# A fused attention and mixture-of-experts kernel: the 1e-9 of two softmax sums becomes a column that tensor_reduce adds, and a table that spreads VectorE's routing work over the attention steps is changed

## The chip, the cores and the metric

The kernel runs on one core of a Trainium2 chip. The metric is the device time of one execution in microseconds (us). The engines are called as in the profile: PE is TensorE (PEld its weight loads), DVE is VectorE, ACT is ScalarE, POOL is GpSimd, SP is the engine that issues nearly all DMAs. Each engine runs its own instructions strictly in the order in which they are written.

## The reference

The reference is windowed attention with a few sink keys, and behind it a two-level mixture of experts over the attention's output. Cut to what matters:

```python
scores = where(keep, q @ k.T / sqrt(D), -1e9)      # B=4, H=8, S=768, D=64, window 128, 4 sinks
a = exp(scores - scores.max(-1))
a = a / (a.sum(-1) + 1e-09)                        # first 1e-9
x = (a @ v) as [3072, 512]
for each token: g = argmax of 4 group logits, e = argmax of that group's 4 expert logits
    g_w = softmax(group logits)[g];  e_w = softmax(expert logits)[e]   # each divides by sum + 1e-9
    out = g_w * e_w * (relu(x @ w1[g, e]) @ w2[g, e])                  # 512 -> 1024 -> 512
```

## The kernel before

**Attention.** The 3072 tokens are 24 tiles of 128 rows. One loop (lines 1081 to 1165) runs 26 iterations i, pipelined three deep: iteration i computes the scores of tile i, transposes and multiplies with the values of tile i-1, and transposes back, normalises and computes routing logits of tile i-2. On PE an iteration is: transposes of tile i-1's probabilities (`tp<-ident,pt`), scores (`ps<-kb,qb`), logits (`lg<-wsd,xT`), two more groups of transposes, values (`po<-pu,vv`, `po<-pa,vv`, `po<-spT,svp`). On DVE it is: minima of the negated scores in two halves (`sm,st<-ps,msk`), the normalised output (`xt<-tp,rc`, function `norm`), and in odd iterations also the normalised logits of two tiles (`lw`, `lt`) and the reciprocals of two tiles' sums (`rc`, function `sums`). So an odd iteration has more fixed DVE work than an even one. ACT computes the exponentials with their row sums, and copies out of PSUM; POOL masks the copied probabilities (affine_select, `pu<-pa`, `pa<-pa`), splits the sink columns (`sp`) and, once in six tiles, subtracts for a split of the sink values (`svp`).

**Routing.** Four batches of 6 tiles. The generator `route_batch` (line 344) yields after each DVE operation or two; `routing(k, ...)` (line 865) runs k such units. At the end of each iteration line 1158 runs `UNITS.get(i, REND)` units, so the table `UNITS` (line 60; 6 where it has no entry) says how many routing operations DVE gets in iteration i. A unit that needs PE first (kind "pe") stops the run until the next iteration. The big operations of a batch are `bf` and `af` (one-hot factors, two of each per batch, counted as two units each); their product on PE (`lg<-af,bf` or `ph<-af,bf`) is added to the table `tab`; `select` then picks the token numbers of an expert (`sel`, `idv`, `gidx`, `idz`, `sidx`), from which POOL gathers rows of x (`xg<-xd,gidx`, line 640). The batch with `pick` 0 chooses the first expert r0, the next one chooses r1 and gives r0's third tile of tokens.

**Weights.** Every expert's two matrices come in 8 chunks of 512 KB (`rw<-in_w`). A chunk is rounded by ACT (`whi`) and its rest is subtracted by DVE (`wlo`, about 1.2 us). `prefetch` (line 656) loads, `wjob` (line 675) rounds. In the loop line 1161 loads one chunk in even iterations from `CHOOK`=14 on and in each of the last three; two iterations later ACT rounds its first half, one iteration after that the second half, and `wlo` follows behind `norm_logits` (the call `late()`, line 1151). So `wlo` stands in iterations 17, 18, 21 and 23.

**Hand-over.** Iterations 24 and 25 have no more scores. `early_work` (line 1068) already feeds PE with the first expert part (r0, 256 tokens): two tiles are transposed (`ph<-ident,xg`), then 8 blocks f of layer 1 run (`ph<-un,whi`, `ph<-un,wlo`, 12 matmuls a block), and behind block 5 (`LATE`) r0's third tile is transposed. From there on experts follow one another, each with its layer 1 and layer 2 on PE.

Of the kernel before, what the change touches and what calls it, by code (L numbers as in the profile page):

```python
# [9 lines left out]
F32 = mybir.dt.float32  # L10
# [4 lines left out]
AF = mybir.ActivationFunctionType  # L15
# [41 lines left out]
XLEAD = 9  # L57
PEGAP = 1.6
REND, TSTEP = 6, 16
UNITS = {7: 3, 9: 3, 10: 9, 15: 3, 16: 9, 17: 5, 21: 3, 22: 9, NI - 1: 2}  # L60
HC = 3
LATE = 5
PELAG = 2.0
# [21 lines left out]
SNAP = 1  # L85
SNAPB = 2
DEPTH = 2
CHOOK = 14
PW = G + NE
WARM = 18  # L90
FILL = [8, 10, 6]
# [40 lines left out]
def moe_attention(tc, kqT, vN, vS, nsw, wgx, w1, w2, out):  # L132
    nc = Pinned(tc)
    v = nc.vector
    with ExitStack() as top, ExitStack() as att:
# [15 lines left out]
        def const(shape, dt, name):  # L151
            return cp.tile(shape, dt, name=name)
# [137 lines left out]
        def other_masks():  # L290
# [3 lines left out]
            v.tensor_tensor(snk[0:D], snk[0:D], isu[0:D], ALU.mult)  # L294
            v.tensor_tensor(mc[0:D, 1], mc[0:D, 1], snk[0:D], ALU.add)

        trib = const([P, P], BF16, "trib")
        rev = const([P, 4], F32, "rev")
        edge = const([P, MAXT + 1], F32, "edge")
# [3 lines left out]
        wsd = const([P, NDC, 2, PW], F32, "wsd")  # L303
        nc.gpsimd.memset(wsd, 0.0)
        def late_consts():
            other_masks()
            nc.sync.dma_start(wsb, wgx.rearrange("(c p) n -> p c n", p=P))
            for j in range(2):
                nc.sync.dma_start(wsd[j * D:(j + 1) * D, :, j],
                                  wgx.rearrange("(c j p) n -> j p c n", j=2, p=D)[j])  # L310
            v.tensor_scalar(colm, col, -float(P), None, ALU.add)
            v.tensor_scalar(trib, diff, 0.0, None, ALU.is_lt)
            v.tensor_scalar(rev, col[:, 0:4], -1.0, 4.0, ALU.mult, ALU.add)
            v.tensor_scalar(edge, col[:, 0:MAXT + 1], float(P), None, ALU.mult)
            v.tensor_copy(val, prti)
            for r in range(NE):
                nc.gpsimd.memset(capt[:, r:r + 1], float(CAPT[r]))
                nc.gpsimd.memset(caps[:, r:r + 1], float(CAPT[r] // P))
            v.tensor_scalar(gen[:, 0:1], win, 1.0, None, ALU.is_lt)
            v.tensor_scalar(gen[:, 1:2], win, float(P), None, ALU.is_gt)  # L320
            v.tensor_scalar(gen[:, 2:3], nsk, float(NSK), None, ALU.is_gt)
            v.tensor_reduce(gen[:, 3:4], gen[:, 0:3], AX.X, ALU.max)
# [21 lines left out]
        def route_batch(i0, nb, lt, wk, pt, tab, na, pick=None):  # L344
            def sm(shape, name, dt=F32):
                return wk.tile([P, MAXB] + shape, dt, name=name, bufs=1)[:, 0:nb]
# [7 lines left out]
            m = sm([nk], "rm")  # L354
            v.tensor_reduce(m, lv, AX.X, ALU.max)
            yield
            d = sm([nk, 4], "rd")
            v.tensor_tensor(d, lv, wide(m), ALU.subtract)
            yield
            o5 = sm([nk, 4], "req")  # L360
# [51 lines left out]
            v.tensor_tensor(av, av, val[:, i0:i0 + nb, None].to_broadcast([P, nb, na]), ALU.mult)  # L412
            yield
            s5 = sm([nk], "rs5")
            v.tensor_reduce(s5, d, AX.X, ALU.add)
            yield
            v.tensor_tensor(m[:, :, 0:G], og, s5[:, :, 1:], ALU.mult)
            yield
            v.tensor_reduce(s5[:, :, 1], m[:, :, 0:G], AX.X, ALU.add)
            ss = sm([2], "rss")  # L420
            v.tensor_scalar(ss, s5[:, :, 0:2], 1e-9, None, ALU.add)
            yield
            v.reciprocal(ss, ss)
            cw = wk.tile([P, MAXB, GW], F32, name="cw", bufs=2)[:, 0:nb]
            v.tensor_tensor(cw, ss[:, :, 0:1].to_broadcast([P, nb, GW]), ss[:, :, 1:2].to_broadcast([P, nb, GW]), ALU.mult)
            gates.extend((i0 + n, cw[:, n]) for n in range(nb))
# [284 lines left out]
        def scores(i, g):  # L711
            t = i % NT
            if g == 0:
                env[i] = e = {}
                e["pt"] = wk.tile([P, H, SW], F32, name="pt", bufs=2)
                if i % 2 == 0:
                    env["st"] = wk.tile([P, 2, 2, H], F32, name="st")
                e["st2"] = env["st"]
                e["st"] = e["st2"][:, :, i % 2]
            m = 3 if t else 2  # L720
            for pp in range(2):
                for j, f in ((0, 0), (1, 1), (0, 1), (1, 0)):
                    d, o = slice(j * D, (j + 1) * D), slice(f * D, (f + 1) * D)
                    end = 2 + 2 * t + f
                    nc.tensor.matmul(psb[g][o, 2 * j + pp, (3 - m) * BW:CW], qb[d, i % NQ, 2 * g + pp, o],
                                     kb[d, end - m:end, 2 * g + pp], start=True, stop=True)
# [4 lines left out]
        def maxima(i, g):  # L731
            t = i % NT
            e = env[i]
            if t:
                v.copy_predicated(psb[g][:, :, CW - D:CW], selu[:, None, :].to_broadcast([P, 4, D]), psb[g][:, :, BW - D:BW])
            e["sm", g] = sm = wk.tile([P, 4, SW], F32, name="sm", bufs=2)
            for k in range(4):
                h = head(g, k)
                v.tensor_tensor_reduce(
                    sm[:, k], psb[g][:, k, CW - SW:CW], msk[:, min(t, 2)], -0.125, 3.0e38,  # L740
                    ALU.add, ALU.min, e["st"][:, 0, h:h + 1])

        def exps(i, g):
            e = env[i]
            for k in range(4):
                h = head(g, k)
                nc.scalar.activation(e["pt"][:, h].rearrange("p (b k) -> p b k", b=2)[:, ::-1],
                                     e["sm", g][:, k].rearrange("p (b k) -> p b k", b=2), AF.Exp, bias=e["st"][:, 0, h:h + 1],
                                     scale=-1.0, accum_out=e["st"][:, 1, h:h + 1])

        def sums(i):
            rc = wk.tile([P, 2, H], F32, name="rc")
            v.tensor_scalar(rc, env[i]["st2"][:, 1], 1e-9, None, ALU.add)
            v.reciprocal(rc, rc)
            for j in range(2):
                env[i - 1 + j].update(rc=rc[:, j], rc2=rc)
# [324 lines left out]
        for i in range(NI + 2):  # L1081
            live = i < NI
            a, b = i - 1, i - 2
            mid, old = 0 <= a < NI, 0 <= b < NI
            state["clk"] += 3.0
            if i == NI:
                state.update(gap=0.0, dve=state["clk"])
                sps.close()
                put_gates(MAXB)
                while later:  # L1090
                    gather(*later.pop(0))
                ps_h = fl.enter_context(tc.tile_pool(name="ps_h", bufs=4, space=PSUM, side="right", reuse_waits="tile"))
                tail.append(ps_h)
                next(ew)
                next(ew)
                if half:
                    half.pop()()()
            if live:
                load_v(i)
            if i == 1:  # L1100
                scores(i, 0)
                scores(i, 1)
            if mid or old:
                env["tp"] = pair()
            if mid:
                trans(a)
                evac(a, 0)
                evac(a, 1)
            if live and i != 1:
                scores(i, 0)  # L1110
            if later and not gates:
                gather(*later.pop(0))
            late = None
            if live:
                if i != 1:
                    scores(i, 1)
                issue()
                warm(FILL[i] if i < len(FILL) else 0, ob[0][:, 224:416])
                late = half.pop()() if half else wjob()
                if half and i % NT == 0:  # L1120
                    late = lambda more=half.pop(): more()()
            if old:
                logits(b)
            if mid:
                sink_t(a)
            if old:
                natural(b)
            if live:
                maxima(i, 0)
                exps(i, 0)  # L1130
            else:
                routing(TSTEP, (None,))
                next(ew, None)
            if mid:
                sink_evac(a)
            if live:
                maxima(i, 1)
                exps(i, 1)
                sink_split(i)
            if i == 0:  # L1140
                late_consts()
            if i % NT == (4 if i else 0) and i < NI - NT + (not i):
                split_s((i + 2) // NT)
            state["clk"] += 3.0
            if old:
                norm(b)
            routing(1, ("pe",))
            if old:
                norm_logits(b)
            if late:  # L1150
                late()
            if mid:
                values(a, 0)
                values(a, 1)
                sink_values(a)
                out_evac(a)
            put_gates(2 if live else MAXB)
            routing(UNITS.get(i, REND) if live else TSTEP, (None, "rd"))
            if live and i % 2:
                sums(i)  # L1160
            if i >= CHOOK and (i % 2 == 0 or i > NI - 4):
                prefetch(min(RAW, len(raws) + (1 if live else RAW)))
            if not live:
                wjob()
                next(ew, None)
# [283 lines left out]
```

## Time and profile before

| | us |
|---|---|
| median of 3 runs (lowest, highest) | 515.48 (514.57, 516.71) |
| the profiled execution | 515.45 |
| span of the profile | 513.7 |
| busy: PE, DVE, ACT, POOL | 495.2, 386.6, 343.9, 160.6 |

The span is what the profiler saw from the first to the last instruction; the profiled execution's own time is 1.75 us longer. Attention ends near 160 us of the span, the experts take the rest. A busy PE in this profile can hide waits, since the ends of matmuls are modelled; the length of a stage is a safer measure.

### The profile page before, as it was taken

Reading aid. Unit: us, or ns where it says so; the run is one execution under the profiler, and the core shown is the slowest. Engines: PE = TensorE matmul, PEld = TensorE weight load, DVE = VectorE, ACT = ScalarE, POOL = GpSimd, SP = SyncE. Lnnn points to the kernel's source line nnn. Section 1 sums busy time; section 2 is a strip of 40 time slices with the busy share of each in tenths; the row PEclk is TensorE's granted clock in tenths of the full one; section 3 lists DMA queues with packets and bytes.
Section 4 is the critical chain, followed back from the end, with each engine's and each line's share of the span. In section 5 each row is a group of like instructions: output and inputs, shape, how many; then the busy total and the mean of one; then the engine's idle time right before and its main releaser. Section 6 shows DMA issues by size and latency. Waiting matters only on the chain. (4 is left out here: it accounts for less than half of the span.)

```text
span 513.7 us, 14666 instructions
## 1 busy us (share of the span) xinstructions
PE 495.2 (96%) x5399; PEld 421.0 (82%) x5399; DVE 386.6 (75%) x1183; ACT 343.9 (67%) x877; POOL 160.6 (31%) x272
## 2 busy tenths in 40 slices
PE   7999999998898999999999999999999999999995
PEld 5788888787687988989888878787779788988884
DVE  7476898898999789985175669847888898788840
ACT  4888878787795445674275667845887887687731
POOL 3464463464365011513304022321253032302101
PEclk9999999999999999999999999999999999999998
DMA  6766775695785645897128379858889797869300
GB/s 199 236 216 218 248 231 183 195 324 178 261 282 150 227 127 173 294 328 266 61 82 301 122 285 305 275 192 286 265 264 323 283 312 229 298 218 332 110 25 27
DMA packets 50000, 114.71 MB, mean 223 GB/s; under 512 B 9486, under 2 KB 9486, under 8 KB 49920
## 3 DMA queue, kind: packets, MB, share of 16 engines
q1 hardware_dynamic: 45424, 100.14, 58.8%
q0 software_dynamic: 4352, 13.26, 7.4%
q8 instruction: 44, 0.72, 0.6%
q10 hardware_dynamic: 144, 0.29, 0.2%
q14 instruction: 36, 0.29, 0.2%
HBM read 100.89 MB, written 13.24 MB: 222 GB/s over the span
## 5 line engine op out<-in xcount | busy, mean ns | idle before, releaser
L102 DVE TENSOR_TENSOR wlo<-rw,whi 128x1024 fp32r<-128x1024 f32 x128 | 153.1, 1218 | 36.5 <-ACT whi L102 35.9
L102 PE MATMUL po<-whi,un 128*128 128x512 f32 (+3 forms) x448 | 148.3, 391 | 0.0
L102 ACT CAST whi<-rw 128x1024 fp32r<-128x1024 f32 (+1 forms) x132 | 131.7, 1023 | 18.0 <-DMA rw<-in_w 12.4
L102 PE MATMUL ph<-un,whi 128*128 128x256 f32 (+4 forms) x576 | 132.3, 317 | 1.0 <-DVE hc L102 0.7
L102 POOL DMA_INDIRECT out<-ot,sidx x33 | 45.3, 1373 | 235.5 <-ACT ot L102 141.4
L102 PE MATMUL po<-wlo,un 128*128 128x512 f32 (+4 forms) x264 | 101.4, 389 | 0.0
L102 PE MATMUL ph<-un,wlo 128*128 128x160 f32 (+4 forms) x416 | 100.6, 267 | 0.0
L102 PEld LDWEIGHTS po<-whi,un 128*128 128x128 f32 (+2 forms) x448 | 79.9, 180 | 22.8
L102 PEld LDWEIGHTS ph<-un,whi 128*128 128x128 f32 x576 | 94.9, 190 | 3.3 <-DVE hc L102 1.2
L102 ACT ACTIVATE pt<-sm,st 128x136 f32<-128x136 f32 x192 | 76.0, 399 | 28.3 <-DVE st L102 28.2
L102 PEld LDWEIGHTS ph<-un,wlo 128*128 128x128 f32 x416 | 77.5, 190 | 0.8
L102 PEld LDWEIGHTS po<-wlo,un 128*128 128x128 f32 (+3 forms) x264 | 43.5, 165 | 12.9
L102 DVE CUSTOM_DVE_ANT_0 sm<-ps,msk 128x136 f32<-128x136 f32 x192 | 45.6, 295 | 3.6 <-PE ps L102 0.8
L102 POOL DMA_INDIRECT xg<-xd,gidx x33 | 34.7, 1050 | 32.5 <-DVE idz L102 20.2
L102 ACT ACTIVATE ot<-po,cg 128x512 f32<-128x512 f32 (+4 forms) x33 | 22.5, 682 | 31.4 <-PE po L102 22.4
L102 PE MATMUL ps<-kb,qb 64*64 64x216 f32 (+1 forms) x768 | 40.9, 353 | 2.0 <-DMA qb<-in_kqT 2.0
L102 DVE TENSOR_TENSOR hc<-ph,hc 128x160 f32<-128x160 f32 (+2 forms) x64 | 22.0, 344 | 23.5 <-ACT hc L102 23.3
L102 ACT ACTIVATE un<-ph 128x256 fp32r<-128x256 f32 (+1 forms) x40 | 15.7, 396 | 35.4 <-PE ph L102 34.6
L102 ACT ACTIVATION_READ_ACCUMULATOR pt<-sm,st 128x1 f32 x192 | 36.3, 189 | 0.0
L102 PEld LDWEIGHTS ps<-kb,qb 64*64 64x64 f32 x768 | 27.8, 140 | 8.2 <-issue 2.4
L102 ACT COPY hc<-ph 128x160 f32<-128x160 f32 (+2 forms) x64 | 19.8, 311 | 19.6 <-PE ph L102 12.6
L102 PE MATMUL po<-pa,vv 128*64 128x64 f32 x768 | 30.8, 223 | 0.5 <-issue 0.5
(187 smaller groups left out, 719.5 us busy)
## 6 DMA issues: line engine op xcount, KB each, us to landing
rw<-in_w SPq DMA_DIRECT2D x128, 512.0 KB, 5.1
vv<-in_vN SPq DMA_DIRECT2D x24, 512.0 KB, 4.2
kb<-in_kqT SPq DMA_DIRECT2D x23, 288.0 KB, 5.0
qb<-in_kqT SPq DMA_DIRECT2D x24, 256.0 KB, 3.4
xd<-xt SPq DMA_DIRECT2D x24, 256.0 KB, 2.6
svr<-in_vS SPq DMA_DIRECT2D x4, 192.0 KB, 4.0
xg<-xd,gidx POOLq DMA_INDIRECT x33, 4.7
out<-ot,sidx POOLq DMA_INDIRECT x33, 5.0
```

The costliest lines, as they stand in the source:

```text
L102: r = f(*a, **k)
```

## The change

Three things are edited. The sums of the exponentials are written by ACT into every other element of a constant tile (`sacc`, three in turn) whose remaining elements POOL sets to 1e-9 once, at the start; `sums` then uses tensor_reduce over the pair in place of tensor_scalar with an addition. In the routing the differences `d` become four of five columns of a constant tile `rdt` with 1e-9 in the fifth, the reduction runs over five columns, and one tensor_scalar per batch goes; the yield there moves up by one operation. The table `UNITS` has other numbers, `CHOOK` is 15, and chunks are loaded in odd iterations.

```diff
-UNITS = {7: 3, 9: 3, 10: 9, 15: 3, 16: 9, 17: 5, 21: 3, 22: 9, NI - 1: 2}
+UNITS = {7: 3, 9: 4, 10: 9, 13: 3, 16: 10, 17: 5, 19: 4, 20: 5, 21: 4, 22: 5, NI - 1: 6}
-CHOOK = 14
+CHOOK = 15
+        sacc = [const([P, 2, H, 2], F32, f"sacc{k}") for k in range(3)]
+        rdt = const([P, MAXB, 1 + G, 5], F32, "rdt")
         def late_consts():
+            for t in sacc:
+                nc.gpsimd.memset(t[:, :, :, 1], 1e-9)
+            nc.gpsimd.memset(rdt, 1e-9)
 ...
-            d = sm([nk, 4], "rd")
+            d5 = rdt[:, 0:nb]
+            d = d5[:, :, :, 0:4]
 ...
-            v.tensor_reduce(s5, d, AX.X, ALU.add)
+            v.tensor_reduce(s5, d5, AX.X, ALU.add)
 ...
             v.tensor_reduce(s5[:, :, 1], m[:, :, 0:G], AX.X, ALU.add)
+            yield
             ss = sm([2], "rss")
-            v.tensor_scalar(ss, s5[:, :, 0:2], 1e-9, None, ALU.add)
-            yield
-            v.reciprocal(ss, ss)
+            v.reciprocal(ss, s5[:, :, 0:2])
 ...
-                    env["st"] = wk.tile([P, 2, 2, H], F32, name="st")
+                    env["st"] = wk.tile([P, 2, H], F32, name="st")
+                e["sum2"] = sacc[i // 2 % 3]
+                e["sum"] = e["sum2"][:, i % 2]
 ...
-                                     scale=-1.0, accum_out=e["st"][:, 1, h:h + 1])
+                                     scale=-1.0, accum_out=e["sum"][:, h, 0:1])
 ...
-            v.tensor_scalar(rc, env[i]["st2"][:, 1], 1e-9, None, ALU.add)
+            v.tensor_reduce(rc, env[i]["sum2"], AX.X, ALU.add)
 ...
-            if i >= CHOOK and (i % 2 == 0 or i > NI - 4):
+            if i >= CHOOK and (i % 2 or i > NI - 4):
```

In the order of instructions this moves work in three places that matter below. The first is DVE in iteration 17, from the normalised output to the end of the iteration. Before:

```order
L102 TENSOR_TENSOR xt<-tp,rc 128x2x4x64
L102 TENSOR_TENSOR lw<-lg,rc 128x320
L102 TENSOR_REDUCE lt<-lw 128x40
L102 TENSOR_TENSOR wlo<-rw,whi 128x1024
L102 TENSOR_TENSOR af_2542<-oh_2066,av_2529 128x336
L102 TENSOR_TENSOR bf<-colm,ga 128x384
L102 TENSOR_TENSOR af_2542<-oh_2066,av_2529 128x336
L102 TENSOR_SCALAR rc<-st 128x16
L102 RECIPROCAL rc<-rc 128x16
```

The same stretch of DVE in the changed kernel:

```order
L102 TENSOR_TENSOR xt<-tp,rc 128x2x4x64
L102 TENSOR_TENSOR lw<-lg,rc 128x320
L102 TENSOR_REDUCE lt<-lw 128x40
L102 RECIPROCAL rss<-rs_2535 128x12
L102 TENSOR_TENSOR cw<-rss 128x96
L102 TENSOR_TENSOR bf<-colm,ga 128x384
L102 TENSOR_TENSOR af_2680<-oh_2207,av_2531 128x336
L102 TENSOR_REDUCE rc<-sacc_178 128x16
L102 RECIPROCAL rc<-rc 128x16
```

The weight remainder `wlo` has left this odd iteration (it now stands in 18, 20, 22, and behind the loop's last live iteration), one `bf` and one `af` of the batch went to iteration 18, and the tail of the batch's gate computation came in. Over the loop the routing operations now stand as follows: three units in 13 (six operations before), the choice of r0 in 15 (14 before), thirteen operations up to the last `rs` in 16, `tab` to `sidx` in 19 (18 before), the first five of the next batch in 20 and its `oh` in 21 (all six in 19 before), eight of the choice of r1 in 22 (ten in 20 before), and seven more operations of that batch in 23.

The second place is PE in the hand-over (iteration 24 and 25). Before, the last block-0 matmuls of r0 are followed by the table product of the third batch, and then by the values of tile 23:

```order
L102 MATMUL ph<-un,whi 128x256 x2
L102 MATMUL ph<-un,wlo 128x256
L102 MATMUL ph<-af_3442,bf 128x112 x6
L102 MATMUL po<-pu_109,vv 64x64 x8
L102 MATMUL po<-pa,vv 64x64 x8
L102 MATMUL po<-pu_110,vv 64x64 x8
L102 MATMUL po<-pa,vv 64x64 x8
L102 MATMUL po<-spT,svp 128x128 x4
```

In the changed kernel PE reaches that product (`ph<-af,bf`) only behind block 2, one iteration later:

```order
L102 MATMUL lg<-wsd,xT 64x40 x8
L102 MATMUL tp<-ident,xT 128x64 x8
L102 MATMUL ph<-un,whi 128x256 x2
L102 MATMUL ph<-un,wlo 128x256
L102 MATMUL ph<-un,whi 128x256 x2
L102 MATMUL ph<-un,wlo 128x256
L102 MATMUL ph<-un,whi 128x256 x2
L102 MATMUL ph<-un,wlo 128x256
L102 MATMUL ph<-un,whi 128x256 x2
L102 MATMUL ph<-un,wlo 128x256
L102 MATMUL ph<-af_3670,bf 128x112 x6
```

Between the product and the transposes of r0's third tile (`ph<-ident,xg 128x128 x4`), which stay behind block 5, PE now has three blocks; before it had the values of tile 23, five blocks, eight logit matmuls and a group of transposes.

The third place is DVE in the same hand-over. Before, the transposed tiles of r0 (`un`) are followed by the last `bf` and `af` of the third batch, and that batch's table is added right behind the next `xt`:

```order
L102 TENSOR_TENSOR un<-ph,un 128x4x128
L102 COPY cg<-xg 128x1
L102 TENSOR_TENSOR bf<-colm,ga 128x384
L102 TENSOR_TENSOR af_3442<-oh_2969,av_3429 128x336
L102 TENSOR_TENSOR xt<-tp,rc 128x2x4x64
L102 TENSOR_TENSOR tab<-tab,ph 128x112
```

In the changed kernel a `wlo` and nine small operations stand between `cg` and this piece:

```order
L102 TENSOR_TENSOR bf<-colm,ga 128x384
L102 TENSOR_TENSOR af_3670<-oh_3247,av_3652 128x336
L102 TENSOR_TENSOR bf<-colm,ga 128x384
L102 TENSOR_TENSOR af_3670<-oh_3247,av_3652 128x336
L102 TENSOR_TENSOR xt<-tp,rc 128x2x4x64
L102 TENSOR_TENSOR wlo<-rw,whi 128x1024
L102 SCALAR_TENSOR_TENSOR un<-ph,un 128x256 x2
L102 TENSOR_TENSOR xt<-tp,rc 128x2x4x64
L102 TENSOR_TENSOR lw<-lg,rc 128x320
L102 TENSOR_REDUCE lt<-lw 128x40
L102 TENSOR_TENSOR tab<-tab,ph 128x112
```

The table is added behind the second `xt` and the last logits. On ACT the second half of the fourth chunk's `whi` now stands in front of the last copies of probabilities (`pa<-tp`). On SP the load of the first chosen expert's number moves one iteration later, and the loads of weights with it.

## Rows read from the trace of the kernel before

**Rows 1.** PE line of the page's slices: busy tenths in 40 slices.

```profile
PE   7999999998898999999999999999999999999995
```

**Rows 2.** Windows per DVE iteration: window, length, busy (instructions) by engine, clock, DMA, GB/s.

```profile
31.42:37.33 5.91, 5.91 (x150) 5.10 (x146) 3.31 (x20) 5.34 (x22) 3.94 (x8) 1.00 0.75 238
37.33:43.08 5.75, 5.75 (x150) 5.07 (x146) 4.75 (x23) 4.84 (x21) 3.43 (x8) 1.00 0.69 219
...
87.23:94.88 7.65, 7.43 (x168) 5.92 (x160) 7.20 (x29) 5.14 (x21) 2.79 (x7) 1.00 0.87 266
94.88:100.41 5.53, 4.74 (x110) 4.04 (x112) 4.58 (x28) 4.68 (x21) 1.15 (x5) 1.00 0.49 164
100.41:106.33 5.92, 5.92 (x150) 5.10 (x146) 5.41 (x28) 5.18 (x21) 3.26 (x8) 1.00 0.70 221
106.33:113.77 7.44, 7.44 (x184) 6.22 (x176) 7.13 (x32) 6.63 (x24) 5.34 (x10) 1.00 0.94 337
113.77:122.54 8.77, 7.31 (x162) 6.33 (x158) 8.52 (x28) 5.58 (x21) 6.23 (x10) 1.00 0.65 216
122.54:129.02 6.48, 5.92 (x136) 4.79 (x133) 4.59 (x25) 5.36 (x21) 1.06 (x4) 1.00 0.54 162
129.02:136.56 7.54, 6.21 (x134) 5.00 (x134) 7.20 (x30) 5.42 (x21) 2.69 (x7) 1.00 0.80 269
136.56:142.10 5.54, 4.85 (x114) 4.12 (x114) 4.86 (x31) 4.69 (x21) 2.29 (x6) 1.00 0.82 246
142.10:148.88 6.78, 6.78 (x168) 5.62 (x160) 6.50 (x27) 6.39 (x23) 5.92 (x10) 1.00 0.92 308
148.88:155.33 6.45, 6.39 (x154) 5.35 (x150) 6.14 (x34) 5.45 (x21) 3.37 (x8) 1.00 0.74 241
```

**Rows 3.** Timeline, iteration 17: start, us, engine, operation.

```profile
121.40 0.91 POOL L102 TENSOR_SCALAR_AFFINE_SELECT pu<-pa 64x512 f32<-64x512 f32 x1
121.71 0.62 DVE L102 TENSOR_SCALAR rc<-st 128x16 f32<-128x16 f32 x1
```

**Rows 4.** Timeline, iteration 10 (the same happens in 16).

```profile
72.61 1.27 POOL L102 TENSOR_TENSOR svp<-svr,svp 32x512 fp32r<-32x512 f32 x1
...
72.66 1.25 DVE L102 TENSOR_SCALAR rss<-rs 128x12 f32<-128x12 f32 x1
```

**Rows 5.** Tiles rc, rs, bf, af on DVE (ns min/median/max), then one timeline row.

```profile
L102 DVE TENSOR_SCALAR rc<-st x12: 153/172/629, 17.7 to 161.5; 128x16 f32<-128x16 f32 x12
...
L102 DVE TENSOR_REDUCE rs<-rd x4: 270/270/271, 71.9 to 181.7; 128x30 f32<-128x120 f32 x4
...
L102 DVE TENSOR_TENSOR bf<-colm,ga x8: 544/550/997, 74.6 to 184.0; 128x384 fp32r<-128x384 f32 x8
...
L102 DVE TENSOR_TENSOR af<-oh,av x8: 496/566/947, 79.6 to 184.5; 128x336 fp32r<-128x336 bf16 x8
...
126.76 1.23 DVE L102 TENSOR_TENSOR wlo<-rw,whi 128x1024 fp32r<-128x1024 f32 x1 [1.40 <-ACT whi L102]
```

**Rows 6.** Timeline of the hand-over, with idle time before; last, landing of tile xg.

```profile
154.48 0.63 ACT L102 CAST whi<-rw 128x512 fp32r<-128x512 f32 x1
...
162.06 0.26 PE L102 MATMUL tp<-ident,sp 64*96 64x64 f32 x2 [1.01 <-ACT pa L102]
...
164.60 0.78 PE L102 MATMUL ph<-af,bf 128*128 128x112 f32 x6
...
165.98 0.26 DVE L102 TENSOR_TENSOR tab<-tab,ph 128x112 f32<-128x112 f32 x1
...
167.12 0.98 POOL L102 DMA_INDIRECT xg<-xd,gidx  x1 [2.69 <-DVE sidx L102]
...
171.91 0.40 PE L102 MATMUL ph<-un,whi 128*128 128x256 f32 x2
...
176.71 0.66 PE L102 MATMUL ph<-ident,xg 128*128 128x128 f32 x4 [0.32 <-DVE un L102]
...
DMA to landing us min/median/max: 2.6/4.7/8.3
```

More of the change, by code (lines that the diff above doesn't have):

```diff
@@ L716, in scores @@
                 if i % 2 == 0:
-                    env["st"] = wk.tile([P, 2, 2, H], F32, name="st")
-                e["st2"] = env["st"]
-                e["st"] = e["st2"][:, :, i % 2]
+                    env["st"] = wk.tile([P, 2, H], F32, name="st")
+                e["st"] = env["st"][:, i % 2]
+                e["sum2"] = sacc[i // 2 % 3]
+                e["sum"] = e["sum2"][:, i % 2]
             m = 3 if t else 2
@@ L740, in maxima @@
                     sm[:, k], psb[g][:, k, CW - SW:CW], msk[:, min(t, 2)], -0.125, 3.0e38,
-                    ALU.add, ALU.min, e["st"][:, 0, h:h + 1])
+                    ALU.add, ALU.min, e["st"][:, h:h + 1])
         def exps(i, g):
@@ L747, in exps @@
                 nc.scalar.activation(e["pt"][:, h].rearrange("p (b k) -> p b k", b=2)[:, ::-1],
-                                     e["sm", g][:, k].rearrange("p (b k) -> p b k", b=2), AF.Exp, bias=e["st"][:, 0, h:h + 1],
-                                     scale=-1.0, accum_out=e["st"][:, 1, h:h + 1])
+                                     e["sm", g][:, k].rearrange("p (b k) -> p b k", b=2), AF.Exp, bias=e["st"][:, h:h + 1],
+                                     scale=-1.0, accum_out=e["sum"][:, h, 0:1])
         def sums(i):
             rc = wk.tile([P, 2, H], F32, name="rc")
-            v.tensor_scalar(rc, env[i]["st2"][:, 1], 1e-9, None, ALU.add)
+            v.tensor_reduce(rc, env[i]["sum2"], AX.X, ALU.add)
             v.reciprocal(rc, rc)
```

## The prediction

> **What bounds the kernel now.** I read the slices of the page first, then the length of each attention iteration as windows cut where DVE starts the first minimum of a tile, then timelines of the long iterations, and last the hand-over to the experts.
>
> The slices [rows 1], 12.8 us each, show PE at 9 tenths and more everywhere between the first and the last one but in slices 10, 11 and 13 (116 to 141 and 154 to 167 us): the second half of the attention part and the hand-over. The expert part runs at PE's pace, so what the change can win lies in the attention part, and what it can lose lies there and in the hand-over.
>
> The windows [rows 2] show why. A plain even iteration takes 5.91 us with PE busy throughout and DVE for 3.31; a plain odd one keeps DVE busy for 4.75. So 5.91 us is PE's pace, and DVE has about 2.6 us to spare in an even and 1.1 in an odd iteration. With routing and weights on top, DVE is busy for 7.20, 7.13, 8.52, 7.20 and 6.50 us in iterations 13, 16, 17, 19 and 21 and those last 7.65, 7.44, 8.77, 7.54 and 6.78: DVE's work plus about 0.3 us. Between them stand iterations with DVE idle (14: 4.58 of 5.53; 18: 4.59 of 6.48; 20: 4.86 of 5.54), whose slack can't be used. Iterations 13 to 22 together last 68.1 us; ten at PE's pace would be 59.
>
> Part of DVE's work is waiting. In iteration 17 tensor_scalar on 16 columns takes 0.62 us while POOL masks [rows 3], and its group spans 153 to 629 ns for one shape [rows 5]; in iterations 10 and 16 tensor_scalar on 12 columns starts 50 ns behind POOL's svp subtraction and ends with it, after 1.25 us [rows 4]. The sum over 120 columns by tensor_reduce took 270 to 271 ns each time [rows 5].
>
> **The change part by part.** *The sums.* Twelve tensor_scalars (median 172 ns) become tensor_reduces over 32 elements. The trace has no such shape; below it is the unblocked 153, above the 270 of 120 elements [rows 5]; I take 0.20, since it has a quarter of those elements. That costs nothing to speak of where it was free and saves up to 0.43 where it was blocked. An odd iteration is then 4.75+0.03, say 4.8. Four tensor_scalars of the gates go as well, but what they waited for stays (below). The Trainium skill (SBUF — State Buffer, "Who interferes with whom") says that on trn2 tensor_reduce never contends with GpSimd, while tensor_scalar can. The trace agrees as far as its constant 270 ns goes.
>
> *The spread over iterations 13 to 22*, each as DVE's new work plus 0.3, or 5.9 where that is less:
> - 13: 4.8 and three operations on 120 columns at 0.27 = 5.6, so 5.9 (was 7.65). 14: 3.3 and the other three = 4.1, so 5.9 (was 5.53, when PE was catching up).
> - 15: 4.8 and the choice of r0, which cost 4.58-3.31 = 1.27 in iteration 14: 6.1, so 6.4 (was 5.92).
> - 16: 3.31, four operations that cost 5.41-4.75 = 0.66 in 15, and nine of those that are there now. Now 7.13-3.31 = 3.82 goes to those nine, the blocked tensor_scalar (1.25), bf (0.55) and two more; 9/11 of the remaining 2.02 is 1.65. Sum 5.6. POOL's svp still runs then; what DVE waits for it lies between nothing and 1.25-0.17 = 1.08, and I take 0.7, since a two-input operation is likely to stand there: 6.6 (was 7.44).
> - 17: 4.8, bf 0.55, af 0.50 and two small ones 0.37 = 6.2; bf and af reached 997 and 947 ns [rows 5], so up to 0.45 more; 6.7 (was 8.77).
> - 18: 4.59 less the six table operations (1.14, by the same six in the hand-over from 165.98 to 167.12 [rows 6]) and plus bf and af 1.05 = 4.5. The 1.40 that wlo waits for ACT's whole whi [rows 5] goes, since both halves are now an iteration apart. Between 4.8 and 5.9; I take 5.4, near the shortest now (was 6.48).
> - 19: 4.8+1.14 = 5.9, so 6.2 (was 7.54). 20: 3.31, wlo 1.23 and five at 0.27 = 5.9, so 6.2 (was 5.54). 21: 4.8 and oh 0.26, so 5.9 (was 6.78). 22: 3.31, wlo 1.23 and eight at 1.27 = 5.8, so 6.1 (was 6.45).
>
> Sum 61.3, that is 6.8 less than 68.1. PE's routing matmuls (0.78 for a table product [rows 6]) come on top of 5.9 where they fall into an iteration at PE's pace; I take off 0.5 for them. Gain 6.3. Its bounds are 9.1, with every iteration at PE's pace, and 2.6, if only 17 loses wlo (1.23) and 18 its wait (1.40). In iterations 7 to 12 only one operation moves, from 10 to 9, and 10 stays blocked by svp: nothing counted.
>
> *The constants.* Four memsets on POOL in iteration 0. A plain iteration leaves POOL 2 us idle [rows 2]; no row shows such a memset, and 512 columns of svp took 1.27, which I take as the most for all four: nothing to 1.3, hidden by that idle time, and if it were not, PE would see it as a late sink split once. I take nothing.
>
> *The hand-over.* Two things are added. First, ACT rounds half a chunk (0.63 [rows 6]) ahead of the last copies pa, and PE's sink transposes already wait 1.01 for pa: 0.6 more, or nothing if pa is early. Behind pa are PE's first block and the values of tile 23; everything waits with it. Second, PE reaches the third batch's table product behind block 2, no longer behind block 0, and needs the third tile of r0 behind block 5. From 171.91 to the end of block 5 (176.71 less 0.32 idle) three blocks take 4.48 [rows 6]. In that time DVE must do the six table operations (1.14 to POOL's issue) and the gather must land, 4.7 median, 2.6 to 8.3. With 0.3 for DVE's logits that stand ahead of the table, the tile is there 6.1 us behind the product and PE waits 1.7; 0.3 of that it waits now. So 1.3 more, between -0.3 and, at 8.3 and 2 us of late DVE, 6.6. Before, values and five blocks hid all this. Later routing (x1, the experts' numbers) moves by about one block and keeps some 10 us of expert work as cover; weights stay eight chunks by then, in the same order. SP's gate stores stand behind a chunk load that waits for a wlo, and that wlo is ahead of the gates on DVE anyway: nothing. Hand-over 2.0.
>
> Sum: 6.3-2.0 = 4.3 off the profiled execution's 515.45, which stands at the median 515.48 of the runs: 511.2.
>
> **The rivals.**
> - *The gather lands in time.* Two of its rows' ends say so: at 2.6 to 3.0 us the tile is there. Then the hand-over costs 0.3, the attention gain is the unshaded 6.8, and the time 509.0. Against it: the median 4.7.
> - *The waits pass on.* The blocked operations are those that overrun into POOL's masking; if DVE's list still overruns, bf, af, cw and oh block instead. bf and af up to 997 ns [rows 5] speak for it, and svp is still there. Then only 17 and 18 gain: 2.6-2.0, so 514.9. The skill (same page and section) states it as a rule: a DVE instruction with two SBUF inputs contends with a GpSimd instruction that reads SBUF. The trace bears that out by bf and af at twice their shortest. Against it: in iterations within 5.9 us none of these is late.
> - *Slower: DVE bounds the hand-over.* There a wlo (1.23), eleven small operations (2.0) and one more bf and af (1.05), 4.3 in all, come ahead of the xt of tile 22, and the transposes of tile 23 need the bank that this xt reads. If nothing hides them and the gather takes 8.3, PE loses 4.3+2.0+3.6 = 9.9 against 6.3: 519.0. It decides from a hand-over above 8.9 us. Against it: PE has the first block, the values and block 1 ahead of those transposes, some 5 us.
>
> **How the numbers follow.** Forecast 0.5 (509.5 to 513), gather in time 0.2, waits pass on 0.2, slower 0.1. Half a per cent, 2.6 us, is about what a measurement of this kernel can tell from no change; the bounds are 512.9 and 518.1. Faster: 0.2 and 0.43 of the forecast's 0.5; within: 0.07 and 0.2; slower 0.1. The range 508.0 to 515.6 leaves out the slower case and a little of the fastest.
>
> **What would show it.** In the changed kernel's profile: no tensor_reduce of rc above 0.3 us; iterations 13, 17, 19 at or below 6.2, 6.9 and 6.4; wlo in 18, 20 and 22 with no wait above 0.5 for ACT; the first block of r0 some 5.5 us earlier; then PE idle for 1 to 3 us ahead of the transposes of r0's third tile, released by a DMA or by ACT's copy of it, and the rest of the trace shifted by a constant. It would be wrong if iterations 13 to 22 still sum to over 65 us, or if the wait at that third tile is over 5.

## The result and the profile after

| | before | changed |
|---|---|---|
| median of 4 runs (lowest, highest) | 516.10 (514.57, 517.83) | 509.08 (506.60, 511.52) |
| the profiled execution, its span | 515.45, 513.7 | 511.52, 509.8 |

The ratio is 0.9867 (95% interval 0.983 to 0.9904). A second measurement of the changed kernel, beside the last experiments, gave 511.03 us against 516.42, ratio 0.9894 (0.9876 to 0.9911). The forecast was 511.2. The medians gained 7.0 and 5.4 us where the forecast had 4.3. The profiled execution of the first measurement is the slowest of its four runs, that of the second (509.01) the fastest of its six, so the two profiles are read side by side below.

The slices of the changed kernel, PE and the granted clock:

```profile
PE   7999999999998999999999999999999999999995
PEclk9999999999998999999999999999999999999999
```

Slices 10 and 11, which were short of 9 in [rows 1], are full; between the first slice and the last only slice 13, the hand-over, is not, and its clock is lower too. The windows by DVE iteration, 13 to 22, answer to [rows 2] (columns as there):

```profile
85.20:91.07 5.87, 5.65 (x126) 4.49 (x118) 5.52 (x27) 5.14 (x21) 1.14 (x4) 1.00 0.87 251
91.07:96.61 5.54, 5.54 (x142) 4.85 (x138) 4.05 (x24) 4.70 (x20) 2.88 (x8) 1.00 0.89 283
96.61:103.01 6.40, 6.40 (x164) 5.56 (x160) 5.95 (x31) 5.15 (x22) 3.13 (x8) 1.00 0.58 201
103.01:110.08 7.07, 7.07 (x174) 5.88 (x166) 6.80 (x33) 6.11 (x23) 4.97 (x10) 1.00 0.70 238
110.08:116.78 6.70, 6.40 (x158) 5.51 (x156) 6.42 (x29) 5.44 (x21) 3.72 (x8) 1.00 0.81 271
116.78:121.75 4.97, 4.87 (x110) 4.10 (x112) 4.51 (x21) 4.69 (x20) 2.70 (x6) 1.00 0.86 329
121.75:128.29 6.54, 6.54 (x138) 5.31 (x130) 6.15 (x30) 6.33 (x23) 1.47 (x6) 1.00 0.68 214
128.29:134.35 6.06, 6.00 (x142) 5.08 (x140) 5.85 (x26) 5.22 (x21) 2.97 (x7) 1.00 0.95 312
134.35:140.47 6.12, 5.66 (x138) 4.98 (x138) 4.91 (x25) 5.05 (x21) 3.82 (x8) 1.00 0.78 236
140.47:146.88 6.41, 6.41 (x162) 5.58 (x158) 5.64 (x29) 5.68 (x23) 4.22 (x9) 1.00 0.83 269
```

Ten iterations last 61.7 us where they lasted 68.1. Behind the length a row has the busy times of PE, PEld, DVE, ACT and POOL. By the third of them no iteration holds 7 us of DVE work any more. The idle DVE time of 18 and 20 is nearly used up (4.51 of 4.97 and 5.85 of 6.06 us); 14 holds less DVE work than before (4.05 for 4.58) and lasts as long (5.54). The tiles rc and rs on DVE answer to [rows 5] (ns min/median/max):

```profile
L102 DVE TENSOR_REDUCE rc<-sacc x12: 171/176/186, 16.4 to 152.8; 128x16 f32<-128x32 f32 x12
...
L102 DVE TENSOR_REDUCE rs<-rdt x4: 296/298/302, 70.7 to 177.3; 128x30 f32<-128x150 f32 x4
```

The reduction for rc never takes more than 186 ns, while the tensor_scalar before it took up to 629. The wait did not all vanish, though. Timeline of iteration 10 of the changed kernel, which answers to [rows 4], then of 16:

```profile
71.60 1.27 POOL L102 TENSOR_TENSOR svp<-svr,svp 32x512 fp32r<-32x512 f32 x1
71.71 1.28 DVE L102 TENSOR_TENSOR cw<-rss 128x96 f32<-128x96 f32 x1
...
107.94 1.27 POOL L102 TENSOR_TENSOR svp<-svr,svp 32x512 fp32r<-32x512 f32 x1
107.95 1.31 DVE L102 TENSOR_TENSOR av<-av,val 128x42 f32<-128x42 f32 x1
```

The next operation with two operands in SBUF, cw or av, now ends with svp (cw takes 0.26 in iteration 17). Last, the hand-over, which answers to [rows 6]; then two windows of it:

```profile
152.87 0.64 ACT L102 CAST whi<-rw 128x512 fp32r<-128x512 f32 x1
153.55 0.40 PE L102 MATMUL tp<-ident,pt 64*128 64x64 f32 x5 [0.81 <-issue]
154.07 1.07 ACT L102 COPY pa<-tp 128x512 f32<-128x512 f32 x2 [0.56 <-PE tp L102]
155.28 0.26 PE L102 MATMUL tp<-ident,sp 64*96 64x64 f32 x2 [0.74 <-ACT pa L102]
165.40 0.78 PE L102 MATMUL ph<-af,bf 128*128 128x112 f32 x6
166.75 0.26 DVE L102 TENSOR_TENSOR tab<-tab,ph 128x112 f32<-128x112 f32 x1
167.90 0.98 POOL L102 DMA_INDIRECT xg<-xd,gidx  x1 [9.71 <-DVE idz L102]
171.37 0.63 PE L102 MATMUL ph<-ident,xg 128*128 128x128 f32 x4 [0.92 <-DMA xg<-xd,gidx]
```

```profile
146.88:171.37 24.49, 22.02 (x331) 20.22 (x325) 21.13 (x71) 12.13 (x35) 7.25 (x12) 0.93 0.65 201
155.94:159.35 3.41, 3.41 (x30) 3.19 (x31) 3.27 (x11) 0.53 (x2) 2.10 (x4) 0.50 0.89 321
```

From the start of iteration 23 to the transposes of r0's third tile PE needs 24.5 us, where it needed 21.4 (155.33 in [rows 2] to 176.71 in [rows 6]). In 3.41 us of that the granted clock was 0.50, that is the 1.2 GHz level, and block 0 took 2.70 us (155.72 to 158.42) where a later block takes 1.47 (166.01 to 167.48). Ahead of that fall PE had been idle twice, 0.81 and 0.74 us; no run here shows where the first of these pauses comes from.

### The profile page after: what moved, and what is told of

Its sections match the earlier page's. It is cut to its first block, busy times and chain, and to the rows that moved or that the text cites. A ratio compares the mean times of both kernels' runs of the same rounds, so it can differ in the third digit from the quotient of the medians.

```text
span 509.8 us, 14665 instructions
## 1 busy us (share of the span) xinstructions
PE 494.3 (97%) x5399; PEld 420.7 (83%) x5399; DVE 382.6 (75%) x1179; ACT 344.1 (68%) x877; POOL 157.2 (31%) x276
## 5 line engine op out<-in xcount | busy, mean ns | idle before, releaser
L102 POOL DMA_INDIRECT out<-ot,sidx x33 | 42.9, 1300 | 234.7 <-ACT ot L102 140.0
L102 POOL DMA_INDIRECT xg<-xd,gidx x33 | 36.7, 1113 | 37.5 <-DVE idz L102 26.6
L102 ACT ACTIVATE ot<-po,cg 128x512 f32<-128x512 f32 (+4 forms) x33 | 22.4, 680 | 35.5 <-PE po L102 26.1
L102 PE MATMUL ps<-kb,qb 64*64 64x216 f32 (+1 forms) x768 | 39.8, 346 | 2.1 <-DMA qb<-in_kqT 2.1
L102 POOL TENSOR_SCALAR_AFFINE_SELECT pu<-pa 64x512 f32<-64x512 f32 x40 | 27.5, 686 | 15.1 <-ACT pa L102 14.8
```

The costliest lines, as they stand in the source:

```text
L102: r = f(*a, **k)
```

## The experiments

The kernels were timed in three groups, 4 to 12 runs of each, always beside the kernel before on the same chip: e1 to e4 (median of the kernel before 515.67 us), e5, e6, e8 and e9 (514.81), and after_again, e10 and e11 (516.42). Across groups the ratios are the better comparison. Of some edits only the lines that matter are shown.

**Only the sums** (e1_sums). The kernel before with tensor_reduce for the sums, the old table and the old loads.

```diff
 ...
-            v.tensor_scalar(rc, env[i]["st2"][:, 1], 1e-9, None, ALU.add)
+            v.tensor_reduce(rc, env[i]["sum2"], AX.X, ALU.add)
 ...
```

> The kernel before with the two 1e-9 columns and tensor_reduce, but with the old UNITS table and chunks loaded in even iterations. Theory A (the spread of DVE's work makes the gain): the iterations stay overlong, the two-input operations still wait for POOL, only the waits of rc in iterations 11, 13, 17 and 19 go (0.43 us each, those of 10 and 16 pass on to cw): 1.7 us, ratio 0.997 (0.994 to 1.000). Theory B (the removed tensor_scalars make the gain, since they no longer block): most of the 6.9 us, ratio 0.990 or less.

Measured: 514.28 us, ratio 0.996 (0.993 to 0.999), as Theory A. In the trace every rc takes 170 to 186 ns. Iterations 7 to 12 fall from 37.7 to 36.7 us, 13 to 22 from 68.1 to 66.3; other operations are blocked instead (cw 0.91 in iterations 10 and 16, req 0.73 in 7). In this profile the clock fell to the 1.2 GHz level from 117.6 to 121.0 us, which hides part of it.

**Only the table and the loads** (e2_table). The kernel before, with its tensor_scalar, and the new table and loads.

```diff
-UNITS = {7: 3, 9: 3, 10: 9, 15: 3, 16: 9, 17: 5, 21: 3, 22: 9, NI - 1: 2}
+UNITS = {7: 3, 9: 4, 10: 9, 13: 3, 16: 10, 17: 5, 19: 4, 20: 5, 21: 4, 22: 5, NI - 1: 6}
-CHOOK = 14
+CHOOK = 15
 ...
-            if i >= CHOOK and (i % 2 == 0 or i > NI - 4):
+            if i >= CHOOK and (i % 2 or i > NI - 4):
```

> The kernel before with the new UNITS table and chunks loaded in odd iterations, but with tensor_scalar for both sums. Theory A: rc no longer stands late in iterations 13 to 22, so its tensor_scalar takes its free 0.17 us there and is blocked at most in 7, 11 and 17; ratio 0.987 to 0.990, 5 us or more of the gain. Theory B: little of the gain, 0.996 or more.

Measured: 508.68 us, ratio 0.987 (0.9837 to 0.9902): the whole gain, as Theory A. The tile rc in this kernel, then iteration 13 and the hand-over as windows:

```profile
L102 DVE TENSOR_SCALAR rc<-st x12: 159/172/631, 16.0 to 154.2; 128x16 f32<-128x16 f32 x12
```

```profile
85.92:92.24 6.32, 6.09 (x134) 4.73 (x126) 5.97 (x26) 5.14 (x21) 1.52 (x5) 1.00 0.88 254
...
148.35:170.68 22.33, 20.59 (x330) 18.95 (x324) 21.43 (x72) 12.04 (x35) 7.42 (x12) 1.00 0.72 219
```

The tensor_scalar is still blocked, up to 631 ns, and so 13 takes 6.32 us and not 5.87; 13 to 22 sum to 62.4. The sums are worth 0.75 us there on top of the table, less than the runs can tell. Iterations 7 to 12 fall as well, from 37.7 to 37.0 us: with one operation moved from 10 to 9, rss in 10 is done ahead of svp and takes 0.17 us where it took 1.25, and only cw is blocked (1.07).

**Loads in even iterations** (e3_even_chunks). The changed kernel with the old condition and CHOOK 14.

```diff
-CHOOK = 15
+CHOOK = 14
 ...
-            if i >= CHOOK and (i % 2 or i > NI - 4):
+            if i >= CHOOK and (i % 2 == 0 or i > NI - 4):
```

> The changed kernel with chunks loaded in even iterations again, so that wlo (1.2 us of DVE) returns to odd iterations 17, 21 and 23 and the rounding in 18 is whole again. Theory A: 17 near 7.9, 18 near 6.3, 21 near 6.4, one of 20 and 22 shorter by 0.2: 2 to 3 us lost in the attention part; the hand-over gets 0.6 back, since no half chunk is rounded ahead of its last copies: ratio 0.990 to 0.992. Rival (parity is all of the gain): 0.997 or more. Rival (parity is nothing, PE sets the pace): 0.987.

Measured: 516.50 us, ratio 1.0016 (0.9993 to 1.0039). Theory A is missed by some 5 us. The number is that of the rival that gives parity all of the gain, but the trace shows a reason that neither of them named: iterations 13 to 22 last 61.9 us, no longer than in the changed kernel. The loss is in the hand-over. Its PE and DVE rows, then two windows:

```profile
162.11 0.58 PE L102 MATMUL ph<-un,wlo 128*128 128x256 f32 x1 [3.97 <-DVE wlo L102]
160.41 0.50 DVE L102 TENSOR_TENSOR af<-oh,av 128x336 fp32r<-128x336 bf16 x1
160.83 1.22 DVE L102 TENSOR_TENSOR wlo<-rw,whi 128x1024 fp32r<-128x1024 f32 x1
```

```profile
147.77:176.94 29.17, 23.28 (x330) 20.89 (x327) 22.16 (x71) 12.68 (x35) 7.55 (x12) 0.88 0.52 171
160.00:166.80 6.80, 4.69 (x68) 4.35 (x68) 2.74 (x5) 0.53 (x2) 0.00 (x0) 0.50 0.61 164
```

By the new table r0 is known at the end of iteration 15, no longer of 14. Odd loads then begin at 15, 17 and 19, even ones at 16, 18 and 20, and every chunk after the first is a step late: the remainders stand in 18, 21 and 23, not in 18, 20 and 22. The fourth, which the changed kernel begins inside the loop and subtracts at 154.40, now stands on DVE behind the whole tail of the third batch, up to its last af, and PE waits 3.97 us for it at the end of block 0. In this profile the clock falls to the 1.2 GHz level during that wait and stays there for 6.8 us. The stretch to the third tile takes 29.2 us.

**One more load with even iterations** (e9_even_17). The changed kernel with even loads and one load more in 17.

```diff
-CHOOK = 15
+CHOOK = 14
 ...
-            if i >= CHOOK and (i % 2 or i > NI - 4):
+            if i >= CHOOK and (i % 2 == 0 or i > NI - 4 or i == 17):
```

> The changed kernel with chunks loaded in even iterations and one extra load in 17; the remainders wlo then stand in 18, 20, 22 and the hand-over in front of the last batch's work, exactly where the changed kernel has them. Theory A (loads in even iterations lost the gain only because one chunk fewer was loaded before the hand-over, so that the fourth wlo stood behind a whole batch on DVE and PE waited 3.97 us for it): the wait is gone and the time is that of the changed kernel, 509.1 us (ratio 0.987). Rival B (the loads themselves disturb even iterations, by their DMA traffic or on SP): 512 us or more (0.992 or more), whatever wlo does.

Measured: 509.09 us, ratio 0.9891 (0.986 to 0.9922), as the changed kernel (0.9867 and 0.9894). The fourth wlo again stands ahead of the third batch's tail on DVE; the changed kernel's row, then the one of this kernel:

```profile
154.40 1.22 DVE L102 TENSOR_TENSOR wlo<-rw,whi 128x1024 fp32r<-128x1024 f32 x1
...
155.00 1.22 DVE L102 TENSOR_TENSOR wlo<-rw,whi 128x1024 fp32r<-128x1024 f32 x1
```

PE runs through block 0 without a wait for it. That settles it: what decides is whether the fourth chunk is ready at the hand-over. A remnant of Rival B shows in iteration 18 (116.72 to 122.97, 6.25 us where the changed kernel has 4.97), where wlo again waits for ACT:

```profile
120.94 1.23 DVE L102 TENSOR_TENSOR wlo<-rw,whi 128x1024 fp32r<-128x1024 f32 x1 [1.40 <-ACT whi L102]
```

It is the wait of [rows 5], and 19 gets 0.3 of it back; 13 to 22 last 62.0.

**The old table with odd loads** (e8_old_table). The changed kernel with the first of the two UNITS lines above.

> The changed kernel with the old table of units; sums by tensor_reduce and the loads of chunks in odd iterations stay. Theory A (the table brings most of the gain, by spreading DVE's work; the parity only brings wlo out of 17 and takes ACT's wait away from 18): 17 and 18 fall to about 6.4 and 5.9 us, but 13 stays at 7.2, 19 at 7.1, 22 rises to 7.4; iterations 13 to 22 sum to 64.3 us (66.3 with the sums alone), hand-over as in the kernel with the sums alone; time 512.9 us (ratio 0.9945). Rival B (the loads in odd iterations carry the gain, since with even loads all of it was lost): 509 us (0.987).

Measured: 512.05 us, ratio 0.9943 (0.9921 to 0.9966), Theory A. Windows of 13, 17, 18 and 22:

```profile
85.63:92.84 7.21, 6.99 (x154) 5.50 (x147) 6.75 (x30) 5.14 (x21) 2.41 (x6) 1.00 0.88 247
111.19:117.94 6.75, 6.75 (x173) 6.04 (x169) 6.50 (x27) 5.60 (x22) 4.70 (x9) 1.00 0.55 138
117.94:123.00 5.06, 5.06 (x116) 4.64 (x118) 4.56 (x25) 4.72 (x20) 2.12 (x6) 1.00 0.91 352
142.16:150.21 8.05, 8.00 (x184) 6.37 (x176) 7.77 (x34) 6.34 (x23) 5.24 (x11) 1.00 0.75 250
```

17 and 18 lose 3.4 us of the 15.25 in [rows 2], since wlo has left 17, its wait for ACT has left 18 and rc is free in 17; but 13 stays long and 22 takes the wlo on top of its nine units: 8.05. The sum of 13 to 22 is 64.6 (64.3 expected). The table is worth the other 3 us.

**svp in other iterations** (e4_svp). The changed kernel with POOL's subtraction moved to 6, 12 and 18.

```diff
-            if i % NT == (4 if i else 0) and i < NI - NT + (not i):
-                split_s((i + 2) // NT)
+            if live and i % NT == 0:
+                split_s(i // NT)
```

> The changed kernel with the split of the sink values (ACT's svp cast and POOL's svp subtraction of 1.27 us) moved from iterations 4, 10, 16 to 6, 12, 18, where DVE has room and the next iteration has no masking on POOL. Theory A: cw in 10 (1.28) and av in 16 (1.31) return to 0.26 and 0.20, and the iterations from 6.70 and 7.07 to 5.9 or 6.0: 1.7 us off the changed kernel, ratio to before 0.983 to 0.984. Rival (PE sets the pace there, the wait cost nothing): 0.987.

Measured: 508.18 us, ratio 0.9851 (0.9821 to 0.9882). Windows of iterations 10 and 16:

```profile
67.02:72.93 5.91, 5.91 (x150) 5.09 (x146) 5.52 (x31) 5.08 (x21) 3.15 (x8) 1.00 0.71 228
102.88:108.79 5.91, 5.91 (x150) 5.09 (x146) 5.52 (x34) 5.07 (x21) 3.15 (x8) 1.00 0.67 214
```

They last 5.91 where the changed kernel has 6.70 and 7.07: that blocking was real, and PE's pace is the floor. Iterations 13 to 22 sum to 59.7. Iteration 23 begins 2.1 us earlier; the time shows about 1 of it, within the intervals.

**The third tile one block later** (e5_late6), and **the half chunk behind pa** (e6_half).

```diff
-LATE = 5
+LATE = 6
```

> The changed kernel with r0's third tile transposed behind block 6 of its layer 1 instead of block 5. Theory A (the gather of that tile lands late, and PE's wait of about 1.0 us ahead of these transposes is a real loss): one more block of 1.4 us stands in front of them, the wait is gone, the same point of the expert part comes 1.0 us earlier, time 508.1 us where the changed kernel has 509.1 (ratio to the kernel before 0.985). Rival B (what is lost there is given back by slack in the expert part, since 1.5 us of the lead already fades there): no wait in the trace, but the time stays at 509.1 (0.987).

Measured: 509.09 us, ratio 0.9888 (0.9856 to 0.992). The wait did not go, it moved: PE of this kernel,

```profile
170.38 0.50 PE L102 MATMUL ph<-un,whi 128*128 128x256 f32 x2 [0.70 <-DVE un L102]
```

waits 0.70 us at block 6 for a PSUM bank that DVE has yet to empty (un). DVE does the routing operations and a wlo first. Rival B's time, but another wait than the slack it named.

```diff
-                if half:
-                    half.pop()()()
...
                 evac(a, 0)
                 evac(a, 1)
+            if i == NI and half:
+                half.pop()()()
```

> The changed kernel with the second half of the fourth weight chunk rounded behind the last copies pa on ACT, not ahead of them. Theory A (the half chunk holds back pa, PE's sink transposes and all behind them): pa ends 0.6 us earlier, PE's idle time ahead of the sink transposes falls from 0.74 to about 0.1 us, and the first block of r0 starts 0.6 us earlier; the fourth wlo comes 0.6 to 1 us later on DVE and is still in time for block 0. Time 508.5 us (ratio 0.986). Theory A with the clock: if the drop to the 1.2 GHz level in the changed kernel's hand-over was caused by that idle time, it is gone as well and 1.5 us more are saved, 507.0 (0.983). Rival B: PE waits for that wlo instead, no gain, 509.1 or more (0.987).

Measured: 509.53 us, ratio 0.9896 (0.9868 to 0.9925), no gain. ACT copies pa right when PE hands it over, but PE's own transposes paused 0.53 us ahead of it, and the wait for pa was 0.74 as in the first profile of the changed kernel. That pause keeps the trace from showing what the half chunk costs. No clock fall stood in this hand-over.

**The changed kernel once more** (after_again), **the product early** (e10_product), **both** (e11_both).

> The changed kernel once more, beside the two that follow. Every theory expects 509.1 us (ratio 0.987) and the same order and lengths of iterations. Open is whether the drop of TensorE's clock to its 1.2 GHz level in the hand-over (3.41 us, at about 1.5 us of loss) belongs to this kernel: if it does, it stands again in the hand-over and the stretch from iteration 23 to the transposes of r0's third tile lasts 24.5 us as in the first profile; if it fell there by chance, that stretch lasts 23.1 us, as in the kernels of the same order so far.

Measured: 511.03 us, ratio 0.9894. The stretch to the third tile in this profile:

```profile
146.92:169.31 22.39, 20.14 (x330) 18.65 (x323) 21.34 (x71) 12.03 (x35) 7.37 (x12) 1.00 0.67 208
```

The clock stays full and the stretch takes 22.4 us. So the fall is no fixed part of the kernel, and the 2.1 us between the two profiles are mostly the fall (some 1.6) and the pause of 0.81 on PE, which is not here either; the wait for pa that follows is 0.4 longer here (1.15 for 0.74). The wait at the third tile is there again, now for DVE:

```profile
169.31 0.63 PE L102 MATMUL ph<-ident,xg 128*128 128x128 f32 x4 [1.09 <-DVE un L102]
```

The edit of e10_product:

```diff
-                routing(TSTEP, (None,))
+                routing(TSTEP, (None, "rd") if i > NI else (None,))
 ...
+            if i == NI:
+                state["at"] = 0.0
+                routing(1, ("pe",))
```

> The changed kernel with the table product of the third batch placed ahead of block 1 of r0 on PE, not behind block 2, and the table and the choice of r0's third tile placed ahead of the values of tile 23 on DVE. Theory A (PE waits 0.9 us for the gather of the third tile because the product is reached late): the gather is issued 2 to 3 us earlier, the wait for the DMA is gone, the point of the third tile comes 0.9 us earlier, time 508.2 us (ratio 0.985). Rival B (behind the gather DVE is late by itself, as the wait for un shows that took its place when the transposes stood one block later): PE waits 0.7 to 1 us for un instead, 509.1 us (0.987).

Measured: 509.08 us, ratio 0.9856 (0.9835 to 0.9877), beside 0.9894 for the changed kernel in the same group. PE's rows:

```profile
159.55 0.54 PE L102 MATMUL ph<-af,bf 128*128 128x112 f32 x3
160.44 0.54 PE L102 MATMUL ph<-af,bf 128*128 128x112 f32 x3 [0.35 <-DVE af L102]
169.27 0.66 PE L102 MATMUL ph<-ident,xg 128*128 128x128 f32 x4
```

The gather goes out 1.2 us earlier, and the wait at the third tile is gone, but the tile comes at 169.27 as it came at 169.31: the product now waits for DVE's last af and takes 1.4 us. The span is 507.3 in both profiles, so the trace doesn't show the 2 us between the medians; the verdict stays open.

> The same as the product placed early, and the subtraction svp moved from iterations 4, 10 and 16 to 6, 12 and 18. The move of svp alone made iterations 13 to 22 shorter by 2 us in the trace and the time 0.9 us shorter. Theory A: both add up, 507.3 us (ratio 0.983). Rival B (the product brings nothing): 508.2 us (0.985).

Measured: 507.47 us, ratio 0.983 (0.9807 to 0.9852), the lowest median of the study, as Theory A. It is 3.6 us below the changed kernel of the same group, but its interval overlaps that of e4_svp (0.9851), so what the early product adds to svp's move is not shown.

## Why the prediction was right

The time lay inside the range, and the mechanism is the one forecast: the new table and loads alone give the whole gain (e2_table), and they give it in iterations 13 to 22. But the gain was put too small. By their intervals the two measurements gained 5.0 us and 4.6 us at the least, the forecast had 4.3, and the rival in which the gather lands in time names the first median (509.08) better, with 509.0. The two profiles of the changed kernel, stretch by stretch, against before (us gained):

| stretch | forecast | first profile | second profile |
|---|---|---|---|
| up to iteration 7 | 0 | 1.0 | 0.8 |
| iterations 7 to 12 | 0 | 1.0 | 1.0 |
| iterations 13 to 22 | 6.3 | 6.4 | 6.7 |
| iteration 23 to the third tile | -2.0 | -3.1 | -1.0 |
| third tile to the end | 0 | -1.4 | -1.0 |
| sum (span) | 4.3 | 3.9 | 6.4 |

That the first profile's 3.9 stands so near 4.3 is luck: its hand-over holds a clock fall that the forecast did not have. Without the fall the sum is 6.4, and the two terms that were mis-sized are iterations 7 to 12 (nothing, measured 1.0) and the hand-over (2.0, measured 1.0).

*The spread held.* Forecast 61.3 and 0.5 for PE's routing matmuls, 61.8 in all; measured 61.7 and 61.5. The rule used, DVE's new work plus 0.3 or PE's pace, was right within 0.2 for 13, 15, 17 and 20 and within 0.5 everywhere in the first profile; that the sum is nearer than that is misses cancelling. The two largest overruns are waits passed on: 16 took 7.07, not 6.6, since svp cost DVE its full 1.1 and not 0.7 (e4_svp gives it all back), and 19 took 6.54, not 6.2, by sidx, blocked for 0.64 us. 14 and 18 fell short, 5.54 for 5.9 and 4.97 for 5.4. The 0.5 for PE fits 15 and 22: they last 6.40 and 6.41 with PE busy throughout and DVE for 5.95 and 5.64, half a microsecond above PE's pace, and the matmuls that rank the tokens (lg<-oh, lg<-runb) take 0.56 in each.

*"In iterations 7 to 12 only one operation moves ... nothing counted"* was wrong by 1.0 us. The saving of "up to 0.43" for a blocked rc was not added up for 7 and 11, where rc took 0.63 and 0.62. The sums alone (e1_sums) shorten these iterations by the same 1.0: in 11 rc's 0.45 goes and nothing takes it over, and in 10 svp blocks one operation (cw), where it blocked rss for 1.25 and cw took 0.50 on top. The gain in 10 also comes by the table alone (e2_table, 6.71 for 7.45), so the one operation that moved was worth 0.7 and not nothing; only that in 11 needs the sums. As far as 13 to 22 go, most of the sums' gain is covered by the table (1.8 alone, with a clock fall in it, and 0.75 beside it).

*The waits pass on* was a rival at 514.9, and its mechanism is there (cw, av, req, sidx), its price is not: moving svp away wins 2.0 us of 13 to 22 (61.7 to 59.7 in e4_svp), and the spread wins 6.4 in spite of it. Behind the rows on cw and av: the Trainium skill (SBUF — State Buffer, "Who interferes with whom") says that a DVE instruction with two SBUF inputs contends with a GpSimd instruction that reads SBUF, and that tensor_reduce never does on trn2; both agree here, 1.28 and 1.31 us against 186 ns at most. The same section says that issue order decides who blocks the other; in the hand-over DVE's wlo began first (154.40) and POOL's select took 1.41 us for 0.65:

```profile
154.72 1.41 POOL L102 TENSOR_SCALAR_AFFINE_SELECT pu<-pa 64x512 f32<-64x512 f32 x1 [2.99 <-ACT pa L102]
156.20 0.65 POOL L102 TENSOR_SCALAR_AFFINE_SELECT pa<-pa 64x512 f32<-64x512 f32 x1
```

*The hand-over* cost 1.0 where the clock stayed full, and 1.0, 1.2 and 1.7 in e2_table, e4_svp and e9_even_17, which have the same order there; the forecast had 2.0. Its two terms were both put too high.

The 0.6 for pa behind the half chunk: in after_again pa does follow the half chunk without a break, but from the first transpose of the probabilities to the sink transposes PE needs 2.47 us (152.13 to 154.60), before 2.27 (159.79 to 162.06). That is 0.2, and e6_half won nothing.

The wait at the third tile: 0.9 and 1.1 us, where the forecast had 1.7, 0.3 of which stood there before. The blocks took what was forecast (4.43 from 166.01, forecast 4.48), and so did DVE from the table to POOL's issue (1.15, forecast 1.14). The table came 0.74 behind the product (166.01 to 166.75) and not 0.3. The gather is where it was mis-sized: where PE waited for it, the tile was there 3.5 us behind POOL's issue (167.90 to 171.37; 3.5 in e2_table, 3.4 in e9_even_17), not at the median of 4.7. So it did not land in time, as the first rival had it at 2.6 to 3.0, but nearer to that than to the forecast. And the cause was only half named: DVE's emptying of the PSUM banks is late by about as much, behind six routing operations and a wlo. Take away one (e5_late6, e10_product) and the other, or DVE's af, holds PE in its place. So the third rival, DVE bounds the hand-over, had its mechanism in part and a price near 1, not 9.9.

The 3.1 of the first profile holds the clock fall: 1.2 in block 0 (2.70 for 1.47) and 0.4 in the first values behind it (1.09 for 0.65). Two of the signs that were named were missed by a little: iteration 19 took 6.54 and not 6.4 at most, and the wait at the third tile was 0.92 in the first profile, not 1 to 3, and for DVE in the second.

*Weights "stay eight chunks by then, in the same order"* cost nothing, and that step rested on where the loads stand: e3_even_chunks lost the whole gain with one chunk fewer ahead of the hand-over, and e9_even_17 got it back with one load.

*Start and end* (1.0 or 0.8, and -1.4 or -1.0) stood in no step. In all profiles of this study iteration 7 starts between 48.5 and 50.0 and the stretch from the third tile to the end takes 336.7 to 339.4 us (where it stands behind block 5), without any order by the edits; no cause was sought.

## What to carry to other kernels

Where one engine sets the pace and another feeds it in steps, write the second one's busy time for each step beside the first one's pace: the excess over the pace, summed, is what a better spread can win. Here the ten iterations came to between 61.0 and 61.9 us in the five profiles that have the changed kernel's order up to there (after, after_again, e5, e6 and e10), forecast 61.8, with single steps off by up to 0.7 either way. A move that delays a choice (which expert) delays what hangs on the choice (its weights); count what is ready at the next hand-over, since one late chunk there cost about as much as ten better steps had won. And where a wait is removed and the time stays, look which engine is late in more than one thing: here the wait went to its next product.

## What was not expected of the hardware

A scalar_tensor_tensor with two operands in SBUF is blocked by POOL like a tensor_tensor: iteration 7 of the changed kernel, where req takes 0.71 us and 0.28 elsewhere.

```profile
53.82 0.65 POOL L102 TENSOR_SCALAR_AFFINE_SELECT pu<-pa 64x512 f32<-64x512 f32 x1 [0.45 <-ACT pa L102]
53.89 0.71 DVE L102 SCALAR_TENSOR_TENSOR req<-rdt,rev 128x120 f32<-128x120 f32 x1
```

In iteration 7 this took the very place of the blocked rc (0.63 before): there the sums' edit won nothing.

Between the first iterations and the last microseconds the granted clock fell to the 1.2 GHz level in three of the profiles: for 3.41 us in the first profile's hand-over, for 3.4 in iterations 17 and 18 of e1_sums (PE paused 1.39 us up to 115.77, ahead of it), and for 6.8 in e3_even_chunks, beginning within a wait of 3.97. In others (after_again, e5_late6, e9_even_17) a wait of 1.15 us at the same place of the hand-over went by without a fall. What tells these apart was not tried.
